# Second batch loaded by two queues and attended to three MLP units later, in a retention and mixer kernel on one core

## The chip, the cores and the metric

The kernel runs on one core of one Trainium2 chip. Its time is the device time of one execution in microseconds; the median of three executions of the kernel before is 330.27 us (329.49 to 330.52). The profile comes from one more execution, recorded by the hardware profiler.

The core's engines are named as the profile names them: PE (TensorE, matmuls; PEld its weight loads), DVE (VectorE), ACT (ScalarE), POOL (GpSimd) and SP (SyncE, which here only issues transfers). Transfers are issued from SP's queue (q1 in the profile) and from POOL's queue (q0); only POOL's can change the type on the way, from float32 in memory to bfloat16 on the chip. Each engine runs its own instructions in program order and waits for others by semaphores.

## What is computed

Inputs q, k and v have 8 batches, 8 heads, 576 positions and 64 columns, all float32. First a causal attention with decay per head instead of a softmax, then a mixer over positions of rank 32, and an MLP of 512 to 2048 to 512 columns with a residual:

```python
scores = scale * np.matmul(q, k.transpose(0, 1, 3, 2))
gamma = 1.0 - 2.0 ** (-5.0 - np.arange(H))
rel = pos[:, None] - pos[None, :]
Dmat = np.where(rel >= 0, gamma[:, None, None] ** rel[None, :, :], 0.0)
attn = np.matmul(scores * Dmat[None], v)

x = attn.transpose(0, 2, 1, 3).reshape(B, S, H * D)
h = x.transpose(0, 2, 1) @ U @ V
u = x + h.transpose(0, 2, 1)
out = u + np.maximum(u @ w_ch1, 0.0) @ w_ch2
```

## The kernel before

**Tiles.** A batch's 576 positions lie in NB = 5 blocks of up to 128 partitions; the half block of 64 is the last in even batches (0, 2, ..) and the first in odd ones, so that two batches fill 9 whole blocks (a "pair"). Heads are taken in NHP = 4 pairs. `k_sets` and `v_sets` are three sets of bfloat16 tiles (k_all and v_all in the profile) that the batches use in turn; `q_raw` are two sets for q. The first batch's k and q arrive in runs of six positions, cast by POOL's queue (`load_first`, lines 1064 to 1066); its v arrives as float32 in a borrowed tile (`given`, `load_first_v`, lines 1100 to 1113) by SP and is cast as DVE scales it by the decay.

**Second batch.** Its q is issued on POOL's queue by `load_second` (line 224), at the end of the set-up. Its k and v are loaded by SP as float32 into tiles that are free at that time (`load_second_kv`, lines 236 to 275): v into `kv_runs` (`v_given`), k of heads 0 to 5 into `y1_sums` and of heads 6 and 7 into the second pair's u tile (`k_given`, line 228). One DVE copy for each of these tiles reads a piece of w2 and writes into a column that the loads overwrite, so that SP's loads wait until that piece of w2 has landed. For each pair of heads SP then loads k and v; ahead of them come the half blocks (`halves`). POOL copies k pair by pair to bfloat16 (four copies), and then issues the loads of batch 2 (`load_batch(2)`, line 275). DVE scales v on its way to v_all (the step vs).

**The mixer's weights.** U and V for the second batch go by POOL's queue (`load_second_mixer`, lines 1120 to 1123) straight behind `load_second`; V is written four times over the partitions (`copies_of_V`, line 1096, a broadcast with the number of copies as its outermost dimension). A further load of three copies of V into V_sb[0] is issued in `between` (line 1233).

**Order of the early part.** A string, `EARLY` (lines 33 to 61), lists by hand the steps of the first two batches and of the first MLP group, which `step` (lines 630 to 840) turns into instructions in this order on every engine. Steps are `op batch headpair banks..`: `w n` are n warm-up matmuls, `tk` and `tq` transposes of k and q, `ck` and `kk` ACT copies of k, `bk` a transpose back, `exp n` ACT's exponentials of one head pair's decay row (`exp_rows`), `qs` and `vs` DVE's scalings of q and v, `gv` the next first-batch v load, `sc` scores, `ma`, `mb` and `ml` DVE's masks, `st` and `S` the states and their copy, `it` and `nt` values, `xa` and `xb` copies of these to x_t, `dn`, `at`, `ux`, `uv`, `ua`, `ub` the mixer, `hu` and `ha` its first-batch form. `M n` is MLP unit n of the first group of 512 positions (four matmuls; 0 to 15 are the first layer, 16 to 31 the second, four units for each 128 positions), `O n` adds u on DVE to 128 finished positions and stores them by SP; `y`, `R`, `Y`, `Q` are parts of units done ahead. `misc` is `between`, `hv` is `load_second_kv`.

**Set-up.** Before `EARLY` stand memsets and small DVE operations for masks and decays (lines 1125 to 1208) and ACT's exponentials: three `exp_rows` and one `exp_of`; the fourth `exp_rows` is a step of `EARLY`.

**After it.** For each further group of 512 positions (j = 1 to 8) a loop runs its MLP units with the steps of the next batch's attention placed between them, each with a due unit (`attention_steps`, lines 559 to 592). The up products (`mix_up`: one 512-column matmul and a DVE add into u) of the second batch's five blocks are due in group 1 (`late`, lines 847 to 851); among them stand batch 2's own (`mix_up_full` at unit 24 and `mix_up` at 27).

Of the kernel before, what the change touches and what calls it, by code (L numbers as in the profile page):

```python
# [14 lines left out]
class Pinned:  # L15
# [24 lines left out]
    0 3 2; dn 0 1 4; qs 0 3; ux 0 0 3; uv 0 0; S 0 2 ACT; ml 0 2; ua 0 0 ACT; it 0 2 2  # L40
    1; vs 0 3; sc 0 3; at 0 1 ACT; nt 0 2; ux 0 1 3; ma 0 3; xa 0 2 ACT; st 0 3 4; xb 0
    2 ACT; mb 0 3; uv 0 1; S 0 3 ACT; ux 0 2 0; dn 0 2 1; ua 0 1 ACT; ml 0 3; it 0 3 2
    4; at 0 2 DVE; y 0 0; nt 0 3; y 0 1; xa 0 3 ACT; xb 0 3 DVE; uv 0 2; y 2 0; ua 0 2
    ACT; ux 0 3 3 1; dn 0 3 2; y 2 1; at 0 3 ACT; y 2 2; y 0 2; uv 0 3; y 1 0; ua 0 3
    ACT; ub 0 3 DVE; y 1 1; y 1 2; y 2 3; y 1 3; R 2; y 0 3; hu 4 4; hu 2 0; R 0; ha 4;
    hu 1 2; hu 0 1; hu 3 3; R 1; M 3; ha 1; ha 2; M 4; R 3; misc; M 5; R 4; M 6; R 5; M
    7; R 6; M 8; ha 0; R 7; ha 3; M 9; R 8; M 10; R 9; M 11; R 10; M 12; R 11; hv; M 13;
# [17 lines left out]
def kernel(  # L65
# [22 lines left out]
    P = 128  # L88
# [1051 lines left out]
    for hp in range(1, NHP):  # L1140
        decays(hp)
# [182 lines left out]
```

## Time and profile before

| what | us |
|---|---|
| median of 3 executions (lowest, highest) | 330.27 (329.49, 330.52) |
| the profiled execution | 330.99 |
| its span, first to last instruction | 329.3 |
| PE busy in the span | 312.2 |
| DVE busy | 230.1 |
| POOL busy | 154.6 |
| ACT busy | 151.9 |

The page of the profile divides the span into 40 equal slices of 8.2 us; a digit is the busy share of a slice in tenths. PEclk is the TensorE clock granted by its throttle, in tenths of full speed. Rows of a timeline give start and length in us, engine, line, operation, what it writes and reads, the number of instructions and, in brackets, the idle time before and what ended it. Nearly all rows carry line 25, that of the helper which passes on every instruction, so the tiles tell them apart: ps_y are the MLP's banks, ps_b those of the early attention, ps_h the up products', w_sb the MLP's weights. A matmul's end is modelled; consecutive ones overlap a little in the rows.

### The profile page before, as it was taken

How to read it: one execution, taken by the hardware profiler on the slowest of the kernel's cores; microseconds unless marked ns; L12 is line 12 of the kernel's file. 1: busy time of each engine (PE TensorE's matmuls, PEld its weight loads, DVE VectorE, ACT ScalarE, POOL GpSimd, SP SyncE). 2: the span in 40 equal slices, each digit the busy share in tenths (PEclk: the TensorE clock that was granted, in tenths of full speed). 3: DMA queues.
4: the chain of work that ended last, by engine and by line, in shares of the span. 5: the costliest groups of instructions: out<-in, count | busy, mean ns of one | idle time of the engine just before them, and what ended most of it. 6: DMA issues, size and time to landing. Idle time of an engine off the chain costs nothing.

```text
span 329.3 us, 9765 instructions
## 1 busy us (share of the span) xinstructions
PE 312.2 (95%) x4136; PEld 207.3 (63%) x4136; DVE 230.1 (70%) x531; ACT 151.9 (46%) x313; POOL 154.6 (47%) x193
## 2 busy tenths in 40 slices
PE   5999939999998999999999999999999999999994
PEld 2764414665543566875588888656877785585483
DVE  7776305757789699978978897888779782253244
ACT  5676501347842167317721771277047605604610
POOL 8382204989990499957696975000400040040040
PEclk9799976999999999999999999999999999999999
DMA  7999997999999699999999999990230034003003
GB/s 119 180 187 206 200 176 174 157 173 129 115 183 149 114 141 162 151 217 121 153 113 207 145 137 99 210 146 2 66 129 2 5 74 135 0 13 117 0 2 128
DMA packets 153580, 40.66 MB, mean 123 GB/s; under 512 B 137920, under 2 KB 152512, under 8 KB 153536
## 3 DMA queue, kind: packets, MB, share of 16 engines
q0 software_dynamic: 89568, 16.96, 68.0%
q1 hardware_dynamic: 63968, 23.08, 35.2%
q8 instruction: 32, 0.52, 0.7%
q14 instruction: 12, 0.10, 0.1%
HBM read 37.44 MB, written 9.44 MB: 142 GB/s over the span
## 4 chain that ended last, share of the span: by engine, by line
PE 74%; DVE 21%; DMA 2%; issue 2%; ACT 0%; DVEq 0%
PE ps_y L25 59%; DVE S L25 8%; PE ps_b L25 7%; DVE ret L25 6%; PE xh L25 3%; DMA kv_runs<-in_v_dram 2%; DVE o_sb L25 2%; DVE y_sums L25 1%; PE sc L25 1%; PE ps_h L25 1%; DVE u_t L25 1%; PE ps_at L25 1%; PE pss L25 1%; DVE qT_all L25 1%; DVE v_all L25 1%
## 5 line engine op out<-in xcount | busy, mean ns | idle before, releaser
L25 PE MATMUL ps_y<-uT_t,w_sb 128*128 128x512 bf16 (+3 forms) x768 | 131.3, 326 | 0.0
L25 ACT ACTIVATE y_t<-ps_y 128x512 bf16<-128x512 f32 x144 | 85.7, 598 | 58.5 <-PE ps_y L25 57.3
L25 PEld LDWEIGHTS <-w_sb 128*128 128x128 bf16 x768 | 68.1, 98 | 49.5 <-DVE uT_t L25 0.6
L25 POOL TENSOR_TENSOR o_sb<-o_sb,u_t 128x512 f32<-128x512 f32 (+1 forms) x24 | 24.4, 1036 | 105.2 <-DVE o_sb L25 104.7
L25 PEld LDWEIGHTS <-y_t 128*128 128x128 bf16 x576 | 55.8, 99 | 20.6 <-issue 3.9
L25 PE MATMUL ps_y<-w_sb,y_t 128*128 128x256 bf16 (+1 forms) x352 | 59.7, 319 | 0.0
L25 DVE SCALAR_TENSOR_TENSOR S<-S,keep,pss 128x64 bf16<-128x64 bf16 x168 | 47.0, 280 | 5.1
L25 DVE TENSOR_TENSOR o_sb<-ps_y,o_sb 128x512 f32<-128x512 f32 x35 | 24.2, 691 | 26.2 <-PE ps_y L25 13.4
L25 DVE TENSOR_TENSOR ret<-sc,qsrow 128x640 bf16<-128x640 f32 x48 | 37.3, 818 | 6.5 <-PE sc L25 4.6
L25 PEld LDWEIGHTS <-y_sums 128*128 128x128 bf16 x336 | 32.0, 98 | 5.1
L25 POOL DMA_DIRECT2D q_all<-in_q_dram x37 | 29.1, 798 | 6.4 <-DMA w_sb<-in_moe_w_ch_dram 5.4
L25 POOL TENSOR_TENSOR v_all<-v_all,vs 128x512 bf16<-128x512 bf16 (+1 forms) x25 | 27.3, 1093 | 7.0 <-DMA v_all<-in_v_dram 5.9
L25 DVE TENSOR_TENSOR y_sums<-y_t 128x512 bf16<-128x512 bf16 x28 | 13.2, 473 | 22.1 <-ACT y_t L25 22.1
L25 PE MATMUL ps_y<-w_sb,y_sums 128*128 128x256 bf16 x224 | 27.3, 273 | 0.0
L25 PE MATMUL ps_y<-kv_runs,y_t 128*128 128x256 bf16 x224 | 27.1, 273 | 0.0
L25 POOL DMA_DIRECT2D k_all<-in_k_dram x30 | 26.7, 891 | 0.6 <-DMA k_all<-in_k_dram 0.4
L25 ACT CAST S<-pss 128x64 bf16<-128x64 f32 x24 | 5.0, 210 | 46.0 <-issue 41.5
L25 ACT ACTIVATE x_t<-xh,xs 128x320 bf16<-128x320 f32 x48 | 22.7, 524 | 7.3 <-PE xh L25 6.3
L25 POOL DMA_DIRECT2D v_all<-in_v_dram x30 | 25.9, 864 | 0.0
L25 DVE TENSOR_TENSOR u_t<-ps_h,x_t 128x512 bf16<-128x512 f32 (+1 forms) x35 | 22.1, 682 | 0.4
L25 PEld LDWEIGHTS <-k_all 64*64 64x64 bf16 (+2 forms) x584 | 11.7, 112 | 9.6 <-POOL k_all L25 5.3
L25 DVE TENSOR_TENSOR y_sums<-y_sums,y_t 128x512 bf16<-128x512 bf16 x28 | 14.1, 505 | 1.0
(130 smaller groups left out, 308.8 us busy)
## 6 DMA issues: line engine op xcount, KB each, us to landing
out_dram<-o_sb SPq DMA_DIRECT2D x36, 256.0 KB, 2.5
w_sb<-in_moe_w_ch_dram POOLq DMA_DIRECT2D x8, 512.0 KB, 12.2
k_all<-in_k_dram POOLq DMA_DIRECT2D x24, 128.0 KB, 5.9
v_all<-in_v_dram POOLq DMA_DIRECT2D x24, 128.0 KB, 6.9
q_all<-in_q_dram POOLq DMA_DIRECT2D x20, 128.0 KB, 5.0
q_all<-in_q_dram POOLq DMA_DIRECT2D x12, 144.0 KB, 5.9
given<-in_v_dram SPq DMA_DIRECT2D x8, 128.0 KB, 4.8
kv_runs<-in_v_dram SPq DMA_DIRECT2D x8, 128.0 KB, 3.4
```

The lines of the kernel that those rows point to most:

```text
L25: return self._tc.keep_in_program_order(call(*args, **kwargs))
```

## The change

Four things are changed.

1. In the set-up, `load_first_v(0)` stands after the fourth doubling of the position row and not before it; `load_first_v(1)`, the zeros of the half block of v and those of U and V stand behind the decay arithmetic and not ahead of it. Of the exponentials only `exp_rows(0)` stays in the set-up; 1, 2 and 3 are steps of `EARLY` behind the first k copies. The first `vs` stands behind the first scores and one mask.
2. Of the second batch's k, heads 0 to 3 come by SP as float32 as before (two POOL copies); heads 4 to 7 come on POOL's queue, cast on the way, issued in `load_second`. DVE zeroes the other half block in `between`. `load_second_mixer` and the three further copies of V are issued behind POOL's two copies.
3. The second batch's steps begin after unit 21 and not after unit 18; between `qs 1 1` and unit 28 the units stand at other places, among them O 1 and O 2.
4. The late up products are due at 14, 20, 22.8, 28.2 and 26.2 and not at 14, 20, 24.2, 27 and 26; batch 2's last one at 30 and not 27.

```diff
 EARLY = """
-    w 8; tk 0 0 0; exp 3; ck 0 0; w 5; bk 0 0 2; tq 0 0 3; kk 0 0; qs 0 0; gv 0 2; exv; tk 0 1
-    0; vs 0 0; ck 0 1; w 1 1; sc 0 0; mb 0 0; bk 0 1 2; tq 0 1 3; ml 0 0; st 0 0 0; ma 0
+    w 8; tk 0 0 0; ck 0 0; exp 1; w 5; bk 0 0 2; tq 0 0 3; kk 0 0; qs 0 0; gv 0 2; exv;
+    exp 2; w 1 1; sc 0 0; mb 0 0; vs 0 0; tk 0 1 0; ck 0 1; exp 3; bk 0 1 2; tq 0 1 3;
+    ml 0 0; st 0 0 0; ma 0 0; kk 0 1; S 0 0 ACT; qs 0 1; gv 0 3; tk 0 2 1; it 0 0 2 0;
...
-    R 12; M 14; R 13; M 15; R 14; M 16; R 15; M 17; M 18; vs 1 0; M 19; tk 1 0 4; O 0;
-    tq 1 0 2; ck 1 0; st 1 0 0; qs 1 0; tq 1 1 1; S 1 0; M 20; qs 1 1; M 21; vs 1 1; M
-    22; sc 1 0 3 4 0; st 1 1 2; ma 1 0; tk 1 1 1; S 1 1; M 23; mb 1 0; ck 1 1; ml 1 0;
-    tk 1 2 2; vs 1 2; it 1 0 1 0; ck 1 2; M 24; O 1; M 25; sc 1 1 3 4 2; vs 1 3; nt 1 0;
-    M 26; xb 1 0 ACT; mb 1 1; xa 1 0 ACT; M 27; ma 1 1; ml 1 1; it 1 1 0 1; O 2; dn 1 0
-    2; nt 1 1; at 1 0 ACT; tq 1 3 3; xa 1 1 DVE; xb 1 1 ACT; st 1 3 4; st 1 2 2; qs 1 3;
+    11; R 10; M 12; R 11; hv; M 13; R 12; M 14; R 13; M 15; R 14; M 16; R 15; M 17; M
+    18; M 19; O 0; M 20; M 21; vs 1 0; M 22; tk 1 0 4; tq 1 0 2; ck 1 0; st 1 0 0; qs 1
+    0; tq 1 1 1; S 1 0; M 23; qs 1 1; vs 1 1; M 24; O 1; sc 1 0 3 4 0; st 1 1 2; ma 1 0;
+    tk 1 1 1; S 1 1; M 25; mb 1 0; ck 1 1; ml 1 0; tk 1 2 2; vs 1 2; it 1 0 1 0; ck 1 2;
+    M 26; sc 1 1 3 4 2; nt 1 0; M 27; xb 1 0 ACT; mb 1 1; xa 1 0 ACT; O 2; ma 1 1; ml 1
+    1; it 1 1 0 1; dn 1 0 2; nt 1 1; at 1 0 ACT; vs 1 3; tq 1 3 3; xa 1 1 DVE; xb 1 1
+    ACT; st 1 3 4; st 1 2 2; qs 1 3; S 1 3; tq 1 2 0; S 1 2; ux 1 1 1; qs 1 2; M 28; sc
...
     def load_second():
         for hp in range(NHP):
             load_runs(in_runs(q_raw[1]), q, 1, hp)
+        load_halves(pool, k_sets[1], k, H // 2, H)
+        for h in range(H // 2, H):
+            load_head(pool, k_sets[1], k, h)
+
+    def load_halves(engine, x, src, h0, h1):
+        for i in range(2):
+            engine.dma_start(
+                out=x[half(i), 0, h0 + i:h1:2, :],
+                in_=src[1, h0 + i:h1:2, 0:HALF, :].rearrange("h s d -> s h d"),
+            )
+
+    def load_head(engine, x, src, h):
+        engine.dma_start(
+            out=x[:, 1:NB, h, :],
+            in_=src[1, h, HALF:S, :].rearrange("(c p) d -> p c d", p=P),
+        )
...
     def load_second_kv():
...
+        load_halves(sp, k_given, k, 0, H // 2)
         for hp in range(NHP):
...
+            for h in (2 * hp, 2 * hp + 1):
+                if h < H // 2:
+                    load_head(sp, k_given, k, h)
+            if hp == 0:
+                load_halves(sp, v_given, v, 0, H)
+            for h in (2 * hp, 2 * hp + 1):
+                load_head(sp, v_given, v, h)
+        for hp in range(NHP // 2):
+            h = slice(2 * hp, 2 * hp + 2)
+            pool.tensor_copy(out=k_sets[1][:, :, h, :], in_=k_given[:, :, h, :])
+        load_second_mixer()
+        pool.dma_start(out=V_sb[0][R:P, 0:S], in_=copies_of_V(1))
         load_batch(2)
...
-        steps.append((at_mixer + (2.5 if b % 2 else 5), 0, lambda: (
+        steps.append((at_mixer + (2.5 if b % 2 else 5 if b > 2 else 8), 0, lambda: (
...
-            for m, up in enumerate((14, 20, 24.2, 27, 26))
+            for m, up in enumerate((14, 20, 22.8, 28.2, 26.2))
...
-    load_first_v(0)
     decays(0)
...
+        if n == 64:
+            load_first_v(0)
...
-    for hp in range(NHP - 1):
-        exp_rows(hp)
+    exp_rows(0)
...
+    load_first_v(1)
+    for i in range(2):
+        dve.memset(v_first[half(1 - i), NB - 1, i::2, :], 0.0)
+    for x in (
+        U_sb[0][:, :, R:P], U_sb[0][HALF:P, NB - 1, 0:R], V_sb[0][R:2 * R, :],
+        V_sb[0][2 * R:P, :], V_sb[0][0:R, S:SP],
+    ):
+        dve.memset(x, 0.0)
     load_first(1)
...
     load_second()
-    load_second_mixer()
 
     def between():
 
-        pool.dma_start(out=V_sb[0][R:P, 0:S], in_=copies_of_V(1))
         dve.memset(k_sets[0][HALF:P, NB - 1, :, :], 0.0)
+        for i in range(2):
+            dve.memset(k_sets[1][half(1 - i), 0, H // 2 + i::2, :], 0.0)
```

More of the change, by code (lines that the diff above doesn't have):

```diff
@@ L40 @@
[L40 to L45, printed above, removed]
@@ L61 @@
+    1 1 ACT; M 30; ck 1 3; it 1 2 2 3; nt 1 2; sc 1 3 4 1 0; xa 1 2 ACT; xb 1 2 DVE; M
+    31; mb 1 3; ml 1 3; ux 1 2 2; ma 1 3; ux 1 0 3; uv 1 0; O 3; ua 1 0 ACT; it 1 3 0 1;
+    nt 1 3; dn 1 2 4; xa 1 3 ACT; xb 1 3 DVE; Y 0 0; Y 0 1; at 1 2 ACT; dn 1 3 3; uv 1
+    2; at 1 3 ACT; ux 1 3 0 1; ua 1 2 ACT; Y 2 0; Y 2 1; uv 1 3; Y 0 2; ub 1 3 ACT; ua 1
+    3 DVE; Y 2 2; Y 1 0; Y 2 3; Y 0 3; Q 2; Y 1 1; Y 1 2; Y 1 3; Q 0; Q 1
 """
@@ L1147 @@
         dve.memset(qz_bufs[i][:, 0, S:SP], 0.0)
-    load_first_v(1)
-    for i in range(2):
-        dve.memset(v_first[half(1 - i), NB - 1, i::2, :], 0.0)
-    for x in (
-        U_sb[0][:, :, R:P], U_sb[0][HALF:P, NB - 1, 0:R], V_sb[0][R:2 * R, :],
-        V_sb[0][2 * R:P, :], V_sb[0][0:R, S:SP],
-    ):
-        dve.memset(x, 0.0)
     load_first(0)
```

62 lines of the change are left out of this document (16 added, 46 removed).

## The prediction

> **What bounds the kernel now.** I read the page first, then who waited for whom on TensorE, then the chain of waits, then a table of windows. In the 40 slices PE is full nearly everywhere, with two holes: the first slice, and slice 5 (41 to 49 us), where the granted clock also falls and stays low in slice 6.
>
> ```profile
> PE   5999939999998999999999999999999999999994
> PEclk9799976999999999999999999999999999999999
> PE ps_b L25 <- POOL k_all L25: 4.8, 1, 4.8
> PE ps_b L25 <- DVE v_all L25: 0.9, 1, 0.9
> PE ps_h L25 <- DVE u_t L25: 0.8, 1, 0.8
> ```
>
> PE's waits that bear on this change: 4.8 + 0.9 us in slice 5 for the second batch's k and v, and 0.8 us for a late up product. The chain of waits (start, length, what) passes through the slice-5 hole by a DMA:
>
> ```profile
> 27.96 14.35 PE ps_y L25 x67
> 42.30 6.32 DMA kv_runs<-in_v_dram
> 48.80 0.84 DVE v_all L25
> 50.90 4.82 PE ps_y L25 x12
> ```
>
> 67 matmuls in 14.35 us is 0.214 us each: one MLP unit of four costs 0.86 us. Behind the hole 12 of the same matmuls take 4.82 us, 0.40 each. The windows (length, busy time of PE, PEld, DVE, ACT, POOL with instruction counts, clock, DMA share, GB/s) say why:
>
> ```profile
> 42.64:49.68 7.04, 1.33 (x17) 1.03 (x18) 0.88 (x2) 0.69 (x1) 0.72 (x1) 0.66 0.88 168
> 49.68:55.65 5.97, 5.97 (x44) 2.67 (x43) 2.75 (x6) 0.37 (x1) 1.78 (x2) 0.54 0.77 173
> 112.00:329.30 217.30, 211.77 (x2854) 152.15 (x2852) 156.27 (x328) 97.52 (x199) 90.17 (x103) 1.00 0.89 102
> ```
>
> The clock is 0.66 and then 0.54, about half speed over most of both. So the hole costs its own 5.7 us and, behind it, 4.82 - 12 x 0.214 = 2.25 us on 12 matmuls. After 112 us PE is busy 211.77 of 217.30 us: whatever shift leaves this region is carried to the end.
>
> What sets the end of the hole are SP's loads of the second batch:
>
> ```profile
> 36.65 0.20 DVE L25 CAST y_sums<-w_sb 128x30 f32<-128x30 bf16 x1 [2.43 <-DMA w_sb<-in_moe_w_ch_dram]
> 36.88 2.46 SPq L25 DMA_DIRECT2D y_sums<-in_k_dram  x4
> 37.17 0.75 POOL L25 DMA_DIRECT2D V_sb<-in_moe_V_dram  x1 [2.27 <-DMA w_sb<-in_moe_w_ch_dram]
> 39.52 5.52 SPq L25 DMA_DIRECT2D kv_runs<-in_v_dram  x4
> 39.93 0.69 POOL L25 DMA_DIRECT2D V_sb<-in_moe_V_dram  x1 [2.00 <-DMA w_sb<-in_moe_w_ch_dram]
> 46.70 0.72 POOL L25 CAST k_all<-y_sums 128x640 bf16<-128x640 f32 x1 [6.08 <-DMA y_sums<-in_k_dram]
> 43.50:45.50 2.00, 0.00 (x0) 0.00 (x0) 0.00 (x0) 0.00 (x0) 0.00 (x0) 0.86 0.80 124
> 48.60:52.00 3.40, 2.53 (x41) 1.56 (x38) 3.20 (x7) 0.69 (x2) 0.77 (x2) 0.50 0.99 224
> 64.00:72.00 8.00, 8.00 (x136) 5.09 (x131) 5.26 (x11) 2.77 (x7) 7.64 (x12) 1.00 2.27 174
> q0 software_dynamic: 786, 0.60, 128.7%
> ```
>
> They are let go at 36.65 by a piece of w2. The last row is the DMA queue table of 37 to 40 us: only POOL's queue (q0) moves, 0.60 MB of earlier issues; SP's pieces start behind it, after 40. Then the transfers sag to 124 GB/s at 43.5 to 45.5 although both queues have work: this is when the two broadcast V loads (issued 37.17 and 39.93) are under way and SP's issue is stuck (four issues in 5.52 us against four in 2.46). Alone, SP's pieces flow at 224 GB/s (48.6 to 52). The clock of 0.86 in the 2 us to 45.50 puts its fall 0.56 us before the end, at 44.9: 2.3 us after PE went idle.
>
> **The change part by part.** The sum is made against the profiled execution: span 329.3, 330.99 us in all, 0.7 above the median of 330.27.
>
> *Start-up.* Here are ACT's rows, two of DVE and PE's wait:
>
> ```profile
> 3.58 2.27 ACT L25 ACTIVATE qsrow<-qT_all,lngam 128x640 bf16<-128x640 f32 x3 [1.47 <-DVE qT_all L25]
> 8.01 0.62 ACT L25 COPY kvT<-ps_b 128x576 bf16<-128x576 bf16 x1
> 8.29 0.45 DVE L25 COPY masklast<-maskbin 64x64 bf16<-64x64 bf16 x2
> 9.57 0.76 DVE L25 TENSOR_TENSOR qz<-ps_b,qsrow 128x576 bf16<-128x576 bf16 x1 [0.83 <-PE ps_b L25]
> 8.69 0.40 PE L25 MATMUL ps_b<-ident,kvT 128*128 128x128 bf16 x4 [1.75 <-ACT kvT L25]
> ```
>
> The first k copy (8.01) stands behind three exponentials, a wait for values that DVE makes after its memsets, and what follows that; with one exponential ahead of it, it can start about 2 us earlier and PE's 1.75 us wait goes. But the next step, the q scaling on DVE, follows all of DVE's setup, which is only reordered: it ends at 8.74 as now, so the 9.57 can move to 8.74 at best, 0.8 us. Then the first v scaling now comes after a mask that waits for the scores, and the wait moves there. Bounds: 0.8 us won, 1.0 lost (0.8 of v scaling behind the mask, 0.2 of later v issues). I take 0, and this matters little: whatever PE wins before 42.64 it waits longer for v, and a loss up to the 0.9 us of idle left below is covered too.
>
> *Three units ahead of the wait.* Units 20 to 22 move in front: 3 x 0.86 = 2.57 us of PE work into the hole. PE arrives at the k transposes at 42.64 + 2.57 = 45.2 and, with 0.44 for k's (57.74 below) and as much for q's at full clock, is done at 46.1. The store sum O 0, now queued behind DVE's wait for v, goes ahead of it.
>
> *Loads.* In front of the wait POOL's queue loses two U loads and the two V loads and gets six k loads: two halves and four heads, 288 KB = 0.295 MB as written, in short rows; SP loses six. At the 174 GB/s of the 64 to 72 us window, where POOL's queue moves such rows, the six cost 1.7 us. SP's first eight pieces (32 x 2 + 128 x 2 + 64 x 2 + 128 x 2 = 704 KB, 0.72 MB) cost 3.2 us at 224 GB/s. Together from 40.6 (an estimate: POOL's queue alone still moves at 40): 45.5, plus 0.4 to the semaphore, 46. Bounds: 45 (half of POOL's heads behind SP's) and 48.6, where they land now. I take 46, since the sag at 43.5 to 45.5 stands exactly while V is in flight. DVE's v scaling of 0.84 us then runs 46.1 to 47.0. POOL's k copy (0.72 us) for the first heads comes at about 44, ahead of PE. POOL's later copies, then U and V (now behind them, issued near 49), then batch 2's loads: these start earlier than now because POOL has two copies fewer, so nothing later waits for them. Only U could be late:
>
> ```profile
> U_sb<-in_moe_U_dram POOLq DMA_DIRECT2D x2, 32.0 KB, 9.0
> k_all<-in_k_dram POOLq DMA_DIRECT2D x24, 128.0 KB, 5.9
> ```
>
> Issued at about 48.4 behind POOL's second k copy, it is read near 56.5 (by the steps below). Its 9.0 us held a backlog of w pieces; with that again PE would wait 0.9 us for it, with the 5.9 of a k block nothing. I take nothing.
>
> By the Trainium skill, "DMA: Bandwidth & Descriptors", Rules for kernel authors, a copy whose outermost dimension is a broadcast of c copies uses at most c of the 16 engines; that fits the sag, and no row here names engines. Without it the 2.6 us I give to the loads would rest on the sag alone.
>
> *From v to the next common point.* With 0.9 us idle (46.1 to 47.0) the clock should hold. These rows give the steps at full clock:
>
> ```profile
> 55.66 0.57 PE L25 MATMUL ps_b<-qz,kvT 64*128 64x128 bf16 x10
> 56.16 0.51 PE L25 MATMUL ps_b<-v_all,k_all 128*64 128x64 bf16 x20
> 56.88 1.03 PE L25 MATMUL ps_y<-w_sb,y_t 128*128 128x512 bf16 x4
> 57.74 0.44 PE L25 MATMUL ps_b<-ident,k_all 128*128 128x128 bf16 x5
> 60.08 0.57 PE L25 MATMUL ps_b<-qz,kvT 64*128 64x128 bf16 x10
> 60.84 1.90 PE L25 MATMUL ps_y<-w_sb,y_t 128*128 128x512 bf16 x8
> 62.57 0.19 PE L25 MATMUL ps_b<-v_all,ret 128*128 128x64 bf16 x1
> 58.22 0.68 DVE L25 TENSOR_TENSOR o_sb<-ps_y,u_t 128x512 f32<-128x512 f32 x1
> 60.52 1.29 DVE L25 TENSOR_TENSOR ret<-ps_b,maskbin 128x512 bf16<-128x512 f32 x2 [0.88 <-PE ps_b L25]
> ```
>
> States and q transposes 0.9, units 23 and 24 1.7, scores to k transposes 1.2 (55.66 to 56.88), unit 25 0.86, transposes and values 0.5, unit 26 0.86, scores and values 0.76 (60.08 to 60.84), unit 27 0.86: 7.7 us, to 54.7. **A new wait** follows. O 2 (0.68 us) now stands on DVE between the two masks of head pair 1, and waits for unit 27; the second mask (0.65) is queued behind it, and PE's values (step it 1 1) behind the mask with no unit in between: 0.68 + 0.65 + 0.1 = 1.4 us. So that step starts at 56.1 where it started at 62.57: 6.4 us.
>
> *Late up products.* The 0.8 us wait of PE on u_t lies at the fourth of the late ones, whose bank waits for DVE's adds; one of these products now goes ahead of the whole product of batch 2 and two go later, so the adds no longer stand in one row. I take 0.7 (bounds 0 and 0.8); next late there would be the adds themselves, with units beside them.
>
> Sum: 6.4 + 0.7 = 7.1 us, 330.99 - 7.1 = **324 us**.
>
> **The rivals.** *B, the clock still falls.* PE now idles 0.9 us, but another 0.9 us before that are transposes, and the fall came after 2.3 us. If it falls, the 12 matmuls of units 23 to 25 and the states run at half speed: 2.25 + 0.3 = 2.5 us, 326.5. The Trainium skill, "TensorE: Matmul & The Clock Gate", Part 4, has transposes not counting as busy, and Part 1 a free-running window of 3.4 us: by that 1.8 us of 3.4 would be empty, and the outcome would hang on where the window lies.
>
> *C, v comes no earlier.* If the sag is not V's, SP's pieces land at 48.6 as now and PE idles from 46.1 to 49.6 with the clock halved. At half speed states and q transposes take 0.55 more and units 23 and 24 8 x 0.19 = 1.5 more, so 7.7 us becomes 9.8, plus 1.4: the common point at 60.9, 1.7 us won, with the up products 2.4: 328.6. The Trainium skill's "DMA: Bandwidth & Descriptors", Issuing engines are not separate DMA queues, speaks for this: spreading loads over POOL and SP saves issue time only.
>
> *D, slower: SP's pieces queue behind POOL's short rows.*
>
> ```profile
> out_dram<-o_sb SPq DMA_DIRECT2D x36, 256.0 KB, 2.5
> out_dram<-o_sb SPq DMA_DIRECT2D x3, 256.0 KB, 4.6
> ```
>
> SP's stores take 2.5 us to land over the run, but 4.6 at 59 to 75 us, beside POOL's k and v loads. If the last k head, issued near 42.5, lands 6 us later (the 5.9 above), at 48.6, and v's heads behind it by the 3.2 us of SP's pieces, at 52, then by C's working v is scaled at 53, the common point lies at 64.2 instead of 62.57, and less 0.7 that is 0.9 us slower, 332. It decides from v landing after 51.1. Against it: six loads are few, 1.7 us.
>
> **How the numbers follow.** Forecast A 0.52 (324), B 0.20 (326.5), C 0.14 (328.6), D 0.14 (332). From 322 (v at 45, 1 us less idle and less wait at O 2) to 329 holds A, B and most of C. The likeliest one's own range is 322 to 325.5. A measurement tells about 0.3%, 1.0 us, from no change: A, B and nearly all of C are faster, 0.83; 0.06 within, from C's late end and D's early end; 0.11 slower.
>
> **What would show it.** Right: PE's wait on k gone, one of about 1 us on v_all near 46; clock 1.00 from 42 to 56; V in flight after 49; a wait of 1.4 us of PE on DVE's ret; no wait on u_t near 100; the three units ahead of the first k transposes. Wrong: v landing at 48 or later, a clock of 0.5 behind the hole, a start-up later by more than 1 us, or batch 2's k and v late at its first transposes (near 70 us), which would give the gain back there.

## The result and the profile after

The changed kernel takes 327.33 us (median of 19 runs, 325.51 to 329.56) where the kernel before took 330.44 us beside it (19 runs, 328.42 to 332.9): ratio 0.9905, 95% interval 0.9878 to 0.9932, or 3.1 us. The forecast was 324 us. The direction was right and the time lies in the range, but less than half of the expected 7.1 us arrived.

The profiled execution took 327.27 us, span 325.6. The slices of PE and of its clock, from the page:

```profile
PE   7799988999999989999999999999999999999994
PEclk9799999999999999999999999999999999999999
```

In this execution the hole of slice 5 is closed and the clock does not fall behind it. PE's waits (total, times, longest) show what stands in its place:

```profile
PE ps_b L25 <- DVE ret L25: 1.7, 2, 1.4
PE ps_b L25 <- DVE qz L25: 1.2, 1, 1.2
PE pss L25 <- DVE v_all L25: 1.2, 2, 0.8
PE ps_y L25 <- DVE o_sb L25: 0.7, 1, 0.7
```

The waits on POOL's k_all (4.8 us) and on u_t (0.8) are gone. The 1.2 us put down to qz is the wait for v, since DVE's q scaling is queued behind its scaling of v. The timeline of PE (start, length, what, idle before) has the predicted steps:

```profile
45.55 0.44 PE L25 MATMUL ps_b<-ident,k_all 128*128 128x128 bf16 x5
47.54 0.51 PE L25 MATMUL ps_b<-v_all,k_all 128*64 128x64 bf16 x20 [1.17 <-DVE qz L25]
56.80 0.41 PE L25 MATMUL ps_b<-v_all,ret 128*128 128x64 bf16 x8 [1.38 <-DVE ret L25]
```

Step it 1 1, the common point of the prediction, starts at 56.80 instead of 62.57: 5.8 us won where 6.4 were forecast. So the loss is not only there. A table of shifts shows where the rest went. For one and the same ACT instruction it gives the start in a profile less its start in the profile before (us; columns are the times in the kernel before):

```
                30.6   63.3   84.1  110.4  146.1  314.5
changed        +0.49  -5.76  -4.98  -6.13  -4.49  -3.72
after_again    +0.43  -4.38  -4.17  -5.43  -3.07  -3.02
late_old       +1.50  -4.65  -4.65  -4.70  -3.90  -4.26
after_o2       +0.51  -4.36  -3.96  -5.23  -3.88  -4.14
after_novs     +0.45  -2.70  -2.70  -3.97  -4.04  -3.41
start_only     -0.06  -0.14  -0.14  -0.20  +0.10  +0.48
steps_only     -0.29  -1.79  -1.79  -1.84  -1.62  -1.54
uv_only        +1.45  -3.48  -0.59  -0.64  +0.41  +1.23
uv_steps       -0.56  -6.85  -1.22  -1.27  -1.27  -1.80
k_late         +0.43  -6.39  -5.32  -6.58  -4.32  -4.34
k_late_again   +3.04  -5.62  -4.98  -6.25  -2.36  -1.80
k_late_novs    +0.46  -7.99  -3.33  -4.59  -4.58  -4.21
q_late         +0.44  -3.75  -3.75  -4.88  -4.87  -1.79
k_late_q       +1.49  -7.47  -4.63  -5.90  -5.59  -2.92
act5           +0.49  -2.67  -2.67  -3.94  -3.93  -4.30
k_late_act     +1.46  -5.91  -3.88  -5.14  -5.22  -5.54
```

In the changed kernel 0.8 us are lost by 84 us and regained by 110, then 1.6 are lost to 146 and 0.8 more to the end: 2.0 us of 5.8 are given back behind the point at which the prediction's sum ends. The first 0.8 us are a wait of PE (0.78 us, at 78.73) for batch 2's v, whose scaling on DVE took 1.60 us from 77.08 on, where the same step takes 0.82 in the kernel before, while POOL scaled v beside it (last section). (The row after_again is a second profile of the same kernel; the other rows are the experiments below.)

What PE waits for in the largest of these losses, again its timeline:

```profile
137.15 1.91 PE L25 MATMUL ps_y<-kv_runs,y_t 128*128 128x256 bf16 x16 [0.71 <-DVE o_sb L25]
139.38 1.92 PE L25 MATMUL ps_y<-w_sb,y_sums 128*128 128x256 bf16 x16 [0.31 <-DVE y_sums L25]
142.02 1.24 PE L25 MATMUL ps_y<-uT_t,w_sb 128*128 128x512 bf16 x5 [0.31 <-DMA uT_t<-u_t]
```

DVE's o_sb in turn waits for POOL's sums. POOL's timeline from the landing of batch 2's turned u to those sums, in the kernel before:

```profile
111.52 0.19 POOL L25 COPY landed<-uT_t 128x4 bf16<-128x4 bf16 x1 [13.29 <-DMA uT_t<-u_t]
...
133.56 4.25 POOL L25 DMA_DIRECT2D q_all<-in_q_dram  x5
137.78 3.69 POOL L25 TENSOR_TENSOR o_sb<-o_sb,u_t 128x512 f32<-128x512 f32 x4
```

and in the changed kernel:

```profile
107.19 0.19 POOL L25 COPY landed<-uT_t 128x4 bf16<-128x4 bf16 x1 [12.61 <-DMA uT_t<-u_t]
...
111.81 1.60 POOL L25 TENSOR_TENSOR v_all<-v_all,vs 128x512 bf16<-128x512 bf16 x1
...
129.95 1.04 POOL L25 TENSOR_TENSOR v_all<-v_all,vs 128x512 bf16<-128x512 bf16 x1 [1.14 <-DMA v_all<-in_v_dram]
130.95 4.25 POOL L25 DMA_DIRECT2D q_all<-in_q_dram  x5
135.18 4.67 POOL L25 TENSOR_TENSOR o_sb<-o_sb,u_t 128x512 f32<-128x512 f32 x4
```

Between these two rows POOL has hardly an idle moment. It starts the chain 4.3 us earlier than before, its sums only 2.6, while PE is 5.9 earlier (x_t at 132.3 us of the kernel before). So POOL, off the critical path before, becomes a bound there.

### The profile page after: what moved, and what is told of

It reads as the page before. It is cut to its first block, busy times and chain, and to the rows that moved or that the text cites. A ratio compares the mean times of both kernels' runs of the same rounds, so it can differ in the third digit from the quotient of the medians.

```text
span 325.6 us, 9745 instructions
## 1 busy us (share of the span) xinstructions
PE 308.3 (95%) x4120; PEld 205.8 (63%) x4136; DVE 230.9 (71%) x530; ACT 151.8 (47%) x313; POOL 158.0 (49%) x197
## 4 chain that ended last, share of the span: by engine, by line
PE 72%; DVE 19%; DMA 4%; issue 3%; ACT 1%; SPq 1%; DVEq 0%; ACTq 0%
PE ps_y L25 58%; DVE S L25 6%; PE ps_b L25 6%; DVE ret L25 5%; PE xh L25 4%; DMA uT_t<-u_t 2%; DMA kv_runs<-in_v_dram 2%; PE sc L25 1%; DVE o_sb L25 1%; DVE v_all L25 1%; DVE y_sums L25 1%; PE ps_h L25 1%; PE ps_at L25 1%; PE pss L25 1%; DVE qT_all L25 1%
## 5 line engine op out<-in xcount | busy, mean ns | idle before, releaser
L25 POOL TENSOR_TENSOR o_sb<-o_sb,u_t 128x512 f32<-128x512 f32 (+1 forms) x24 | 25.4, 1080 | 105.9 <-DVE o_sb L25 105.4
L25 PEld LDWEIGHTS <-y_t 128*128 128x128 bf16 x576 | 55.1, 98 | 18.9 <-issue 0.9
L25 PE MATMUL ps_y<-w_sb,y_t 128*128 128x256 bf16 (+1 forms) x343 | 55.9, 310 | 0.8 <-issue 0.5
L25 DVE TENSOR_TENSOR o_sb<-ps_y,o_sb 128x512 f32<-128x512 f32 x35 | 24.2, 691 | 27.9 <-PE ps_y L25 12.8
L25 POOL DMA_DIRECT2D k_all<-in_k_dram x36 | 30.7, 855 | 9.7 <-DMA w_sb<-in_moe_w_ch_dram 7.7
L25 DVE TENSOR_TENSOR y_sums<-y_t 128x512 bf16<-128x512 bf16 x28 | 14.0, 501 | 22.1 <-ACT y_t L25 22.1
L25 DVE TENSOR_TENSOR o_sb<-ps_y,u_t 128x512 f32<-128x512 f32 (+1 forms) x16 | 10.3, 650 | 7.6 <-PE ps_y L25 7.6
L25 PEld LDWEIGHTS <-ret 128*128 128x128 bf16 (+1 forms) x320 | 11.9, 98 | 5.9 <-DVE ret L25 2.5
```

Of the source, the lines that this page charges most:

```text
L25: return self._tc.keep_in_program_order(call(*args, **kwargs))
```

## The experiments

Each kernel ran beside the kernel before on the same chip; ratios are to it.

### The parts alone

**uv_only**: U and V behind POOL's copies of k, all else as before.

```diff
     load_second()
-    load_second_mixer()
...
-        pool.dma_start(out=V_sb[0][R:P, 0:S], in_=copies_of_V(1))
...
+        load_second_mixer()
+        pool.dma_start(out=V_sb[0][R:P, 0:S], in_=copies_of_V(1))
         load_batch(2)
```

> The kernel before with one part of the change: the second mixer's U and V loads go out behind POOL's copies of k. This asks the prediction's loads term by itself. Theory 1 (as predicted: the broadcast V loads cause the sag of the transfers): from SP's gate to the landing of v's eighth piece 9.1 us instead of 11.7, PE's idle time in the hole 2.6 us less, time about 2.6 us less, 327.8. Theory 2 (all transfers share one first-come order, and V was only a part of what lay ahead): 10.5 to 11.2 us from the gate to the landing, 0.5 to 1.2 us less, 329.2 to 329.9. Rival: V lands too late for the second batch's up product, a new wait near 100 us, 330.4 or more.

Measured: 330.74 us, ratio 1.0033 (1.0008 to 1.0058). The loads, from the timelines of SP's queue and DVE:

```profile
37.52 2.45 SPq L25 DMA_DIRECT2D y_sums<-in_k_dram  x4
40.16 3.16 SPq L25 DMA_DIRECT2D kv_runs<-in_v_dram  x4
...
46.37 0.82 DVE L25 TENSOR_TENSOR v_all<-kv_runs,vscale 128x640 bf16<-128x640 f32 x1 [7.00 <-DMA kv_runs<-in_v_dram]
```

From SP's first issue to the v scaling it takes 8.85 us instead of 48.80 - 36.88 = 11.92: the loads of U and V cost SP's pieces 3.1 us, where theory 1 had 2.6, and theory 2's 10.5 to 11.2 is refuted. This run moves U and V together, so that V's share is not separated. But the time did not follow, which neither theory had; it is the rival's, though its wait near 100 us did not come. PE's timeline shows why:

```profile
74.62 0.23 PE L25 MATMUL psk<-ident,k_all 128*128 128x128 bf16 x1 [1.21 <-DMA k_all<-in_k_dram]
75.88 0.23 PE L25 MATMUL psk<-ident,k_all 128*128 128x128 bf16 x1 [1.03 <-DMA k_all<-in_k_dram]
```

U and V now stand ahead of batch 2's loads, and PE waits 2.2 us for that batch's k. A further 1.9 us are lost behind 110 us; their cause was not followed.

**steps_only**: the order of the first steps from `hv` on as in the change, loads and start-up as before (the diff is the second half of EARLY's).

> The kernel before with one part of the change: the second batch's steps behind three more MLP units (the order from hv on), loads and start-up as before. Theory: v lands 11.7 us behind the gate as before, PE reaches the k transposes 2.6 us later and idles about 3 us instead of 5.7, the clock still falls (low for 3.4 to 7 us), step it 1 1 starts 1 to 2 us earlier than at 62.57; time 328.5 to 329.5, so that about half of the change's gain is in this part. Rival 1: the units are worth all of their 2.57 us, or more because the clock holds: 327.8 or less. Rival 2: the clock falls later and takes the units behind with it, no gain: 330.4.

Measured: 330.26 us, ratio 1.0002 (0.998 to 1.0023). This is the time of rival 2. PE's timeline and a window (length, busy of PE, PEld, DVE, ACT, POOL, clock, DMA, GB/s):

```profile
47.15 0.57 PE L25 MATMUL ps_b<-ident,k_all 128*128 128x128 bf16 x5 [2.22 <-POOL k_all L25]
49.27 0.74 PE L25 MATMUL ps_b<-v_all,k_all 128*64 128x64 bf16 x20 [0.93 <-DVE qz L25]
...
60.77 0.41 PE L25 MATMUL ps_b<-v_all,ret 128*128 128x64 bf16 x8 [1.38 <-DVE ret L25]
47.30:54.20 6.90, 5.97 (x63) 3.06 (x63) 3.72 (x7) 1.06 (x2) 1.51 (x2) 0.51 0.72 163
```

The hole shrinks by 2.6 us, but the clock is still at 0.51 for 6.9 us behind it, and O 2's new wait takes 1.4: it 1 1 is 1.8 us earlier in the profile, and the medians show nothing of it.

**start_only**: the new order of set-up and first steps alone.

```diff
+        if n == 64:
+            load_first_v(0)
...
-    for hp in range(NHP - 1):
-        exp_rows(hp)
+    exp_rows(0)
```

> The kernel before with one part of the change: the start-up (memsets and exponentials behind the first copies, the new order of the first steps), everything else as before. Theory (the prediction's term of zero): what PE wins or loses at the start it waits less or more for v: 330.4 within 0.6. Rival 1: PE's start is 0.4 us later and the DMA order behind it too, 330.8 to 331.5. Rival 2: the first loads and with them SP's gate come 0.9 us earlier, as the one profile of the changed kernel had it: 329.5.

Measured: 330.9 us, ratio 1.0017 (0.9998 to 1.0037): the predicted zero lies in the interval, if barely. A loss of up to 1.2 us, and so rival 1's time, is not excluded; its profile shows none (at 30.6 us it is 0.06 us earlier).

**late_old**: the changed kernel with the late up products where they were.

```diff
-        steps.append((at_mixer + (2.5 if b % 2 else 5 if b > 2 else 8), 0, lambda: (
+        steps.append((at_mixer + (2.5 if b % 2 else 5), 0, lambda: (
...
-            for m, up in enumerate((14, 20, 22.8, 28.2, 26.2))
+            for m, up in enumerate((14, 20, 24.2, 27, 26))
```

> The changed kernel with the late up products due where they were before (14, 20, 24.2, 27, 26, and batch 2's last at 27). Theory 1 (what the second batch won is given back on POOL: the earlier DVE add of a late product holds up batch 2's turned u, on which POOL's loads of group 2 start, and POOL's sums of group 2 come late): PE's 0.8 us wait on u_t near 100 us is back, but POOL's first instruction of group 2 comes 0.6 to 0.8 us earlier than 107.2, PE's waits near 136 to 142 (1.3 us) shrink below 0.5, and the time is within 0.7 us of the changed kernel's 327.3. Theory 2 (the move is a plain gain, as forecast): 0.7 to 0.8 us slower than the changed kernel, 328.1, and the waits near 136 to 142 stay.

Measured: 327.01 us (4 runs), ratio 0.9882 (0.9815 to 0.9949), not told apart from the changed kernel. PE's wait on u_t is back:

```profile
PE ps_h L25 <- DVE u_t L25: 0.8, 1, 0.8
```

yet at 314 us the profile has more of its shift left (4.26) than the changed kernel's (3.72). So by these two profiles what the late up products win near 106 us is worth nothing at the end; the times, with an interval of 2.2 us to either side, cannot tell 0.7 us. Of theory 1 the waits near 137 us are gone as it said, but POOL's first instruction of group 2 came at 107.99 and not ahead of 107.2. As this profile was also 1.1 us later at 63 us, it does not decide between the theories.

**uv_steps**: uv_only and steps_only together, which is the change without the halving of k, the start-up and the late up products.

> The kernel before with two parts of the change together: U and V behind POOL's copies of k, and the second batch's steps behind three more units; k still all by SP and four copies of it on POOL, start-up as before. Theory (POOL is the second bound: with U, V and four copies ahead of them batch 2's loads go out 3 to 4 us later than before, so that what PE wins in the hole it waits for psk's k near 70): step it 1 1 starts about 6 us earlier than at 62.57, then waits of 3 to 5 us of PE on k_all at 66 to 74, and no gain at the end: 329.5 to 331. Rival (the parts add up and the halving of k is worth nothing): 326.5 to 328.

Measured: 330.04 us, ratio 0.9978 (0.9951 to 1.0006). PE's timeline and two windows:

```profile
45.95 0.51 PE L25 MATMUL ps_b<-v_all,k_all 128*64 128x64 bf16 x20 [0.62 <-DVE qz L25]
...
55.21 0.41 PE L25 MATMUL ps_b<-v_all,ret 128*128 128x64 bf16 x8 [1.38 <-DVE ret L25]
...
72.32 0.23 PE L25 MATMUL psk<-ident,k_all 128*128 128x128 bf16 x1 [0.73 <-DMA k_all<-in_k_dram]
73.56 0.23 PE L25 MATMUL psk<-ident,k_all 128*128 128x128 bf16 x1 [1.01 <-DMA k_all<-in_k_dram]
56.00:60.40 4.40, 4.40 (x88) 3.10 (x88) 2.00 (x4) 1.44 (x4) 4.03 (x6) 0.62 0.76 86
74.00:77.50 3.50, 3.50 (x45) 1.40 (x43) 0.83 (x2) 1.81 (x4) 3.35 (x4) 0.52 1.99 127
```

It 1 1 comes at 55.21, 7.4 us earlier and better than my forecast. Some 1.6 us go to a fall of the clock behind O 2's wait (0.62), and 3.6 (the shift goes from 5.30 at 66.9 us to 1.67 at 80.2) to batch 2's k at 72 to 74 us and the clock behind it (0.52). This suggests what the halving of k is for. With four copies on POOL, batch 2's first k load goes out at 58.24; with two, at 53.40 (59.01 in the kernel before):

```profile
52.98 1.30 POOL L25 DMA_DIRECT2D U_sb<-in_moe_U_dram  x2
54.27 1.44 POOL L25 DMA_DIRECT2D V_sb<-in_moe_V_dram  x2
55.70 2.55 POOL L25 DMA_DIRECT2D q_all<-in_q_dram  x4
58.24 0.91 POOL L25 DMA_DIRECT2D k_all<-in_k_dram  x1
```

and the changed kernel:

```profile
48.16 1.28 POOL L25 DMA_DIRECT2D U_sb<-in_moe_U_dram  x2
49.43 1.44 POOL L25 DMA_DIRECT2D V_sb<-in_moe_V_dram  x2
50.86 2.55 POOL L25 DMA_DIRECT2D q_all<-in_q_dram  x4
53.40 0.91 POOL L25 DMA_DIRECT2D k_all<-in_k_dram  x1
```

None of the three parts that were run alone (uv_only, steps_only, start_only) gains anything, and the two that close the hole gain 0.2% together, not clear of no change. What the changed kernel has beyond them is the halving, the start-up and the late up products. The halving was not run alone, so that its worth is argued from these rows.

### The hole again

**after_again**: the changed kernel, nothing edited.

> The changed kernel once more, for a second profile of it. Theory: v's eighth piece lands 10.4 to 10.8 us behind the gate again, PE idles 1 to 2.5 us for v, and whether the clock falls behind it differs between executions; it 1 1 starts 3 to 6 us earlier than at 62.57, and whatever it is, 3.4 to 4.3 us of it are left at the end; time 327.3. Rival (the 5.8 us of the first profile are the rule, and the end follows them): it 1 1 at 56.5 to 57 again.

Measured: 327.67 us, ratio 0.9906 (0.987 to 0.9942). PE's timeline and the window behind the wait:

```profile
46.14 0.45 PE L25 MATMUL ps_b<-ident,k_all 128*128 128x128 bf16 x5 [0.49 <-POOL k_all L25]
48.91 0.51 PE L25 MATMUL ps_b<-v_all,k_all 128*64 128x64 bf16 x20 [1.95 <-DVE qz L25]
...
58.18 0.41 PE L25 MATMUL ps_b<-v_all,ret 128*128 128x64 bf16 x8 [1.38 <-DVE ret L25]
48.90:52.40 3.50, 3.33 (x70) 2.08 (x71) 3.30 (x7) 0.37 (x1) 3.49 (x6) 1.00 0.97 170
```

The first profile was a lucky one. Here PE idles 2.4 us, it 1 1 is at 58.18, and 3.0 us are left at the end, less than the 3.4 to 4.3 expected. Five other kernels below and above have the same code up to there (late_old, after_novs, q_late, dve5, act5), with it 1 1 at 57.91, 59.86, 58.81, 57.74 and 59.89; over the seven profiles the mean gain is (5.77 + 4.39 + 4.66 + 2.71 + 3.76 + 4.83 + 2.68) / 7 = 4.11 us. An eighth, after_o2, has the same code up to the wait. In four of the eight (act5, q_late, after_novs, after_o2) the clock falls behind the wait; in act5:

```profile
49.10:52.40 3.30, 2.96 (x37) 1.79 (x38) 2.37 (x5) 0.37 (x1) 3.30 (x5) 0.50 0.96 191
```

PE's wait for v is 1.95 us in act5, the same as in after_again, where the clock stayed at 1.00. Nor does the length of the wait order the rest: the clock fell behind 1.59 us in q_late and held behind 2.11 in dve5. Of the seven, the four in which it held gain 4.91 us on the mean, the three others 3.05.

**after_o2**: the changed kernel with O 2 behind step it 1 1.

```diff
-    O 2; ma 1 1; ml 1 1; it 1 1 0 1; dn 1 0 2;
+    ma 1 1; ml 1 1; it 1 1 0 1; O 2; dn 1 0 2;
```

> The changed kernel with O 2 put back behind the values of head pair 1 (it 1 1), where it was before. Both theories: PE's wait of 1.38 us at 55.4 us on DVE's ret is gone and the steps behind it come 1.4 us earlier. Theory 1: POOL's chain does not start 1.4 us earlier, so less than 0.8 us of this reaches the end (326.5 to 327.3). Theory 2: all of it does, 325.9.

Measured: 327.18 us (4 runs), ratio 0.9874 (0.9801 to 0.9947). The 1.38 us wait is gone, 0.21 remain. In its profile the clock fell behind a wait of 2.29 us for v, so that it 1 1 comes at 58.20 and does not show the 1.4 us. The time is not told apart from the changed kernel's.

**k_late**, and once more as **k_late_again**: after_o2 with POOL's six k loads behind its first copy of k.

```diff
-        load_halves(pool, k_sets[1], k, H // 2, H)
-        for h in range(H // 2, H):
-            load_head(pool, k_sets[1], k, h)
...
+            if hp == 0:
+                load_halves(pool, k_sets[1], k, H // 2, H)
+                for x in range(H // 2, H):
+                    load_head(pool, k_sets[1], k, x)
```

> The changed kernel with the store sum O 2 behind step it 1 1, and POOL's six k loads issued behind its first copy of k instead of ahead of SP's gate. Theory (POOL's k heads lie ahead of SP's v in one first-come order, and the clock falls in about half of the executions because v lands at 47.6): v's eighth piece lands 1.2 to 1.7 us sooner behind the gate (9.0 to 9.5 us), PE idles under 1.2 us, the clock holds, it 1 1 starts at 55.5 or sooner; time 325 to 326. Rival 1: the k heads do not hold v up (10.5 us as before), time 327.2. Rival 2: the k heads now come late at the transposes of head pair 2, a wait of 1 us or more at 55 to 60: 327.5 or more. Rival 3: the wait is won at the start and given back between 63 and 200 us: 326.5 to 327.

> k_late once more beside the changed kernel, since four runs did not tell the two apart. Theory: 0.4 to 1 us faster than the changed kernel, 326.5, because the hole closes but POOL's chain keeps the end. Rival: no difference.

Measured: 326.75 us (4 runs), ratio 0.9884 (0.9843 to 0.9926); again 325.7 (6 runs), 0.9884 (0.9831 to 0.9937). From SP's first issue to the v scaling it takes 8.15 and 8.86 us, against 10.7 in the changed kernel. Step it 1 1 comes at 56.17 and 56.94, later than the 55.5 expected. The hole closes (6.4 and 5.6 us at 63 us), but by 84 us 5.3 and 5.0 are left, and 1.0 and 2.6 of these are lost to 146 us: rival 3's course. (The profile of k_late_again is of its slowest execution, 329.15 us.) The changed kernel and this one are not told apart by their intervals.

### What takes the gain behind 63 us

**after_novs**, **before_novs** and **k_late_novs**: POOL scales one column of one head of v instead of all, in batches 3 to 7.

```diff
-            out=v_all[lo:hi, m, :, :], in0=v_all[lo:hi, m, :, :], in1=vs_b[lo:hi, m, :, :],
+            out=v_all[lo:hi, m, 0:1, 0:1], in0=v_all[lo:hi, m, 0:1, 0:1],
+            in1=vs_b[lo:hi, m, 0:1, 0:1],
```

> The changed kernel with POOL's scaling of v left out in batches 3 to 7, but for one column of one head, so that POOL's waits for v's loads stay. Theory 1 (the gain is given back by POOL being late and by DVE's 2-byte sums that stand still while POOL scales v): no DVE sum takes over 0.6 us where 0.42 is usual, PE's waits behind 75 us fall from 3.9 us to about 1, and the time falls to 322.5 to 324. Theory 2 (nothing is given back; the stall was worth only 3 us in the usual execution): within 1 us of 327.3.

> The kernel before with the same part left out (POOL's scaling of v in batches 3 to 7, but for one column). Theory 1: it falls by about 1 us only, to 329 to 329.7, so that the changed kernel without this scaling is 5.5 to 7 us faster than this one, which is the 6.4 + 0.7 us of the forecast. Theory 2: the two differ by 3 us as the whole kernels do.

> k_late with POOL's scaling of v left out in batches 3 to 7 but for one column of one head, about 1 us of POOL for each block. Theory (what is given back between 63 and 200 us is POOL's: its chain of loads, scalings and sums is only 3 to 4 us earlier, not 6): the shift at 63 us stays to 146 us within 0.7 us, no wait of PE on DVE's o_sb near 136; end 5.5 to 6 us earlier than the kernel before, 324.5 to 325.5. Rival (the give-back comes from DVE or from the transfers): end as k_late, 4.3 us earlier, 326.5.

Measured: after_novs 327.63 us (4 runs), ratio 0.9883 (0.9799 to 0.9967), no gain over the changed kernel; in its one profile the clock fell behind the hole and only 2.7 us were won at 63 us, so that it cannot show how much of a larger gain would be kept. before_novs 334.79, ratio 1.0119 (1.008 to 1.0158), slower, which no theory had: PE stands still for 2.3 us at 124 us ahead of scores that read the turned q and k; the profile names no releaser, and why is open. k_late_novs 325.13 (6 runs), 0.9812 (0.9764 to 0.9861): the time that the theory gave. Its profile loses 4.4 us to batch 2's k near 70 us, with the clock falling behind it, and nothing of the rest to 146 us.

**q_late** and **k_late_q**: batch 5's q loads on POOL behind its sums.

```diff
+            steps += [(20.5, 9, lambda: load_q(5, range(NB)))]
...
-            load_batch(j + 3)
+            load_batch(j + 3, with_q=j > 2)
```

> The changed kernel with the five q loads of batch 5 on POOL behind group 2's three sums on POOL instead of ahead of them (4.2 us of issues). Theory: PE's three waits at 136 to 142 (0.71, 0.31, 0.31 on DVE's o_sb, which waits for POOL's) are gone, 1.3 us, and what is left of the shift at 146 is 5.8 us; end 1 to 1.3 us better than the changed kernel, 326.2. Rival: the late q loads make the transposes of batch 5 late, or the shift is lost at the next scalings of v beside DVE's sums: 327.3.

> k_late with the same late q loads. Theory: k_late's gain of about 6 us at 63 us is kept to 5 or more at 146: 325 to 325.7, the fastest of all. Rival: as k_late, 326.7.

Measured: q_late 328.85, ratio 0.995 (0.9918 to 0.9982), and k_late_q 328.04, 0.9904 (0.9864 to 0.9944): misses. PE's waits near 137 are gone, but a wait of PE on uT_t comes right behind (1.58 us in q_late, 1.39 in k_late_q), and in q_late two more on o_sb and y_sums at 171 and 174 (0.67 and 0.80). The work is only moved on POOL; that this is why the turned u lands later was not followed.

```profile
142.91 3.40 PE L25 MATMUL ps_y<-uT_t,w_sb 128*128 128x512 bf16 x15 [1.58 <-DMA uT_t<-u_t]
```

**dve5** and **k_late_dve5**: batch 5's v scaled by DVE.

```diff
-            if b < NRUNS:
+            if b < NRUNS or b == 5:
...
-            if b >= NRUNS:
+            if b >= NRUNS and b != 5:
```

> The changed kernel with batch 5's v scaled by DVE (four steps of 0.82 us an MLP tile later) instead of POOL (five of 1.05 us between 109 and 131 us). Theory (POOL's chain from 107 to 140 us takes 1.3 us of the shift): POOL's sums start 4.5 to 5.5 us earlier, PE's waits on o_sb at 136 to 142 are gone, 5.5 us or more of the shift are left at 146; at the end 0.5 to 1.3 us better than the changed kernel, 326 to 326.8. Rival 1 (DVE is as tight): the waits move to DVE's steps behind 165 us, no gain, 327.3. Rival 2: PE's waits near 136 stay, then POOL is not their cause.

> k_late with the same scaling of batch 5's v on DVE. Theory: of the 6 us won at 63 us 5 or more are left at 146 and 4.8 or more at the end: 325.3 to 326, the fastest valid version. Rival: as k_late, 326.7.

Measured: 339.9 us, ratio 1.0296 (1.0249 to 1.0344), and 337.65, 1.0244 (1.0193 to 1.0294). Both do more than move the scalings: the list of blocks to be scaled always keeps two back, and without batch 5 behind them batch 4's last two waited until POOL came to batch 6. Up to there, at 139.9 us, PE has no wait since 117, so that those near 137 are gone.

```profile
144.99 0.27 PE L25 MATMUL pss<-v_all,k_all 64*64 64x64 bf16 x4 [5.14 <-POOL v_all L25]
```

In dve5 PE then waits 3.3 us for DVE's own scalings between 185 and 199 us (rival 1).

**act5**: batch 5's v scaled by ACT, in the products of group 3; the list keeps its order.

```diff
+    def scale_by_act(b, h):
+        x = v_sets[b % NSET][:, :, h, :]
+        act.activation(out=x, in_=x, func=AF.Copy, scale=vs64[:, h:h + 1])
...
+        if b == 5:
+            return
...
+        if j == 3:
+            steps += [(18 + h / 2, 9, lambda h=h: scale_by_act(j + 2, h)) for h in range(H)]
```

> The changed kernel with batch 5's v scaled by ACT (eight steps of about 0.5 us in the products of group 3, where ACT is idle for 10 us) instead of POOL (five of 1.05 us between 109 and 131 us); the queue of scalings keeps its order, so nothing else is moved. Theory (POOL's chain from 107 to 140 us takes 1.3 us of the shift): POOL's sums start about 5 us earlier than in the changed kernel, near 130, PE's waits on o_sb at 136 to 142 are gone, and the shift at 146 is that at 118, within 0.5 us; time 0.5 to 1.3 us better than the changed kernel, 326 to 327. Rival 1: PE's waits near 136 stay: not POOL. Rival 2: they go and come back as waits on kT_all or uT_t, since the transfers are as tight: 327.4.

Measured: 326.83 us (6 runs), ratio 0.9897 (0.9856 to 0.9939), within the theory's bounds, but not told apart from the changed kernel. In the profile PE has no wait of over 0.2 us from 120 us to the end, and of 3.75 us of shift at 118 us 3.93 are there at 146 and 4.30 at the end. POOL's sums start at 134.50, not near 130: POOL's last q loads now wait for transfers, 1.6 us in all. But this profile came only 3.9 us early to 110 us, and late_old, 4.7 us early and with all scalings on POOL, has no wait of PE near 137 either, so that act5 alone does not decide. ACT had the room:

```profile
163.48 3.72 ACT L25 ACTIVATE v_all<-v_all,vs 128x320 bf16<-128x320 bf16 x8
173.82 0.21 ACT L25 CAST S<-pss 128x64 bf16<-128x64 f32 x1 [6.62 <-issue]
```

**k_late_act**: k_late with ACT scaling v in all of batches 3 to 7, so that POOL scales nothing and no work is left out.

```diff
+        if b > 2:
+            return
...
+        if j + 2 < B:
+            steps += [((18 if j > 1 else 23) + h / 2, 9, lambda h=h: scale_by_act(j + 2, h)) for h in range(H)]
```

> k_late with the scaling of v on ACT for all of batches 3 to 7 (in the products of the group two before), so that POOL scales nothing. Theory: as k_late_novs, but with all of the work done: no slow operations of DVE beside POOL's scalings, no waits on o_sb, the shift at 84 us kept to the end; 324.8 to 325.8, about 5 us less than before and faster than both. Rival 1: PE waits for ACT (y_t or x_t queued behind the scalings): 327 or more. Rival 2: batch 2's k becomes the bound near 70 and takes 2 to 4 us with the clock, as in k_late_novs' profile: 326 to 327.

Measured: 324.73 us (6 runs, 322.91 to 325.62), ratio 0.9815 (0.9777 to 0.9852): by the medians 5.3 us faster than the kernel before beside it, and below the changed kernel's interval. It is faster than both; its interval just touches that of k_late (from 0.9843). In its profile PE pays twice for k in the DMA queue, and for nothing of POOL's behind:

```profile
53.45 0.38 PE L25 MATMUL ps_b<-ident,k_all 128*128 128x128 bf16 x4 [1.43 <-DMA k_all<-in_k_dram]
...
72.90 0.23 PE L25 MATMUL psk<-ident,k_all 128*128 128x128 bf16 x1 [1.46 <-DMA k_all<-in_k_dram]
```

What is left at 84 us (3.9) grows to 5.5 at the end. POOL's sums of group 2 start at 132.05 after a wait of 3.4 us for DVE, where in the changed kernel they start at 135.18 without one.

## Why the prediction was right in direction and wrong in size

Of the 7.1 us forecast 3.1 arrived. By the profiles (an estimate, from the mean gain of 4.1 us at it 1 1) about 2.3 of the missing 4.0 are lost in the hole, by SP's pieces and by the clock, and the other 1.7 behind it.

**The loads: right in mechanism, 1.5 us off in size.** That the loads of U and V hold up SP's pieces is shown (uv_only, uv_steps: 3.1 us from the issue to the v scaling); V alone was not run. That POOL's six k loads cost 1.7 us was near: 10.71 us from SP's first issue (35.95) to the v scaling (46.66) in the changed kernel against 8.85 in uv_only is 1.9, and k_late, without these six ahead, has 8.15 and 8.86. The failed term is SP's eight pieces "3.2 us at 224 GB/s", "together from 40.6": I priced them as bytes in a full queue, but in uv_only SP itself needs 5.8 us to issue them (37.52 to 43.32), and v is scaled 8.85 us behind the first issue where the sum without POOL's 1.7 has 7.5. That the issuing sets the landing, and not something else in the queue, is argued. The forecast had v at 46 for a gate at 36.88, 9.2 us to the scaling; both profiles of the changed kernel have 10.7. That v came at 46.5 in the first is due to its gate, 0.9 us earlier than before; the seven other profiles of this code have it at 36.3 to 37.4, about where it was.

**The clock: rival B in half of the profiles.** The prediction said that with 0.9 us idle the clock should hold, and gave the rival a chance of 0.20. In the eight profiles of this code PE waited 1.2 to 2.3 us for v; the clock fell behind it in four (q_late, act5, after_novs, after_o2) and held in four. A fall costs step it 1 1 about 1.5 us (59.89 in act5 against 58.18 in after_again, less the 0.2 by which the wait ends later). By the Trainium skill, "TensorE: Matmul & The Clock Gate", Part 1, the window is free-running; the pair act5 and after_again, with one wait of 1.95 us and two outcomes, agrees.

**The steps to it 1 1: right.** Three units ahead of k, V in flight after 49 us, O 2's wait of 1.38 us (forecast 1.4), U in time, start-up not told from zero (start_only). Forecast 6.4 us, in the two profiles 5.8 and 4.4, mean of seven 4.1. Where the clock held the mean is 4.9: the missing 1.5 are as much as v came later behind its gate than forecast (10.7 against 9.2). The falls of the clock take the mean down by the other 0.8.

**The late up products: the wait went, the gain did not stay.** 0.84 us of PE's wait disappeared as forecast; late_old, without it, is as fast within its interval.

**The step that failed behind the hole** is the sentence behind the windows: "After 112 us PE is busy 211.77 of 217.30 us: whatever shift leaves this region is carried to the end." A busy PE shows that nothing else bounds it now, not by how much. Of 5.8 and 4.4 us won at 63 us, 2.0 and 1.4 are given back, though the late up products put 1.2 on top. The cause of the loss between 110 and 146 us is POOL: its sums reach 135.18 only 2.6 us earlier. This is shown by taking work off POOL: without its scalings the shift of 110 us is kept to 146 us (k_late_act 5.1 and 5.2, k_late_novs 4.6 and 4.6), in k_late_act to the end, and the same kernel with them (k_late, k_late_again) loses 2.3 and 3.9 us there. Kernels with POOL's scalings that came as early as k_late_act, after_o2 and after_again, lose 1.4 and 2.4. One batch's scalings (act5) fit, but that profile came too little early to decide; that moving POOL's work on POOL moves the wait (q_late) fits too. PE's waits near 137 name the sums; how much POOL's scalings add by slowing DVE beside them (below) is not separated. The 0.6 to 1.3 us lost near 190 us are not explained: in the changed kernel DVE's slow additions (below) stand ahead of them, but k_late_novs, without POOL's scalings, loses 0.9 us there too.

**Nothing waits later for batch 2's loads, for the reason given** (two copies fewer on POOL): uv_steps, with four copies, loses 3.6 us there. PE's wait of 0.78 us for batch 2's v at 78.73 was for its scaling, not for its load. The margin is thin, as the kernels that arrive earlier show (k_late_act waits 1.46 us). Rivals C and D did not come: v was 1.2 us quicker behind the gate, and SP's pieces were held up by POOL's rows by 1.9 us, not 6. By the Trainium skill, "DMA: Bandwidth & Descriptors", Issuing engines are not separate DMA queues, spreading loads over POOL and SP saves issue time only; the trace agrees in that the halving of k did not bring v earlier (10.7 us against 8.9), but it spared POOL two copies.

Open: what makes before_novs slower, and how much of the 4 us spread of the changed kernel's 19 runs is the clock.

## What to carry to other kernels

A gain ahead of a busy engine is carried on only as far as the other engines' chains come earlier too: before adding it to the end, measure how early each chain that feeds the bound (here POOL's loads, scalings and sums) would be, and compare its slack with the gain. Price a group of transfers by the issuing engine's time for its pieces as well as by their bytes. Where parts of a change depend on one another, parts alone can each be worth nothing, so test them in pairs.

## What the runs showed of the hardware

DVE's additions of two bf16 tiles (128x512) take 0.42 us, but up to 1.27 us when POOL scales v beside them. Groups of DVE by form (min/median/max in ns), the changed kernel and then k_late_act, where POOL's tensor work is only its sums:

```profile
L25 DVE TENSOR_TENSOR y_sums<-y_sums,y_t x28: 424/425/1274, 116.5 to 310.1; 128x512 bf16<-128x512 bf16 x28
```

```profile
L25 DVE TENSOR_TENSOR y_sums<-y_sums,y_t x28: 424/424/427, 117.4 to 308.3; 128x512 bf16<-128x512 bf16 x28
```

In the changed kernel the slow one starts at 181.98 (1.27 us) and POOL's scaling of 1.04 us at 181.94. The Trainium skill, "Trainium Architecture — The Big Picture", What this means for kernel authors, says that these two engines share a port pair by a lock; the numbers agree, since the addition ends 0.27 us behind POOL's scaling, whose whole length it stood.

DVE's own scaling of v in batch 2 meets the same in the changed kernel:

```profile
L25 DVE TENSOR_TENSOR v_all<-v_all,vs x4: 812/821/1597, 70.6 to 88.9; 128x640 bf16<-128x640 bf16 x4
```

The slow one starts at 77.08 (1.60 us), a scaling of POOL's of 1.06 us at 76.93; PE waits 0.78 us for it.
